# A new order for the first tiles and block one of a chunk-attention and elu-FFN kernel, and three single steps moved later

## The chip, the cores and the metric

The kernel runs on one core of one Trainium2 chip. The metric is the device time of one launch in microseconds (us). Each kernel is run several times; the median of the runs stands for it. One further execution is recorded by the hardware profiler, and all rows quoted below come from it.

## What is computed

Two stages, both in float32. First attention inside chunks of 64 tokens (batch 8, 8 heads, 576 tokens, head size 64), then a feed-forward layer with an elu between two products:

```
scores = scale * q_c @ k_c^T            # per chunk of 64 tokens
attn   = softmax(scores)                # exp(scores - max) / (sum + 1e-9)
x      = (attn @ v_c) as [4608, 512]    # tokens by (head, dim)
h      = x @ w_in                       # w_in  [512, 2048]
g      = where(h > 0, h, exp(min(h, 0)) - 1)
out    = g @ w_out                      # w_out [2048, 512]
```

q, k and v are float32. The two weights reach the kernel as 64-bit floats, seen as pairs of 32-bit words.

## The kernel before

**Blocks and tiles.** The 4608 tokens are nine blocks of 512 (TB); a block is four tiles of 128 (P). Blocks 0 to 2 are done plainly; blocks 3 to 8 are done in three pairs with a seven-product scheme. The change is in block 0 ("block one" in the words of the change), in what comes ahead of it, and at three places behind it.

**Products.** TensorE multiplies in a fast float32 form that keeps fewer bits, so each operand is split into a high part and the rest, and each product is three matmuls (`three`, L419: high by high, high by low, low by high). `hidden(f)` (L428) makes one 128x512 tile of h from four slices of the contraction: 12 matmuls. One hidden slice f of 16 then goes through `elu` (L436), a generator with four steps, each an "e" in the order strings: ScalarE takes relu and exp (L439, L440); VectorE joins them with a maximum (L442); ScalarE casts the high part ghi (L447); VectorE subtracts to get glo (L450). Then four groups of three matmuls add the slice to the four output tiles (`second_products`, "P", 12 matmuls). So one f is "H", four "e" and one "P".

**Weights.** In blocks 0 and 1 the split weights are used from SBUF, and block 0 must make them. A unit u (`load_unit`, L109) is slice u of w_in and slice u-1 of w_out, 512 KB each, loaded into one of three `st` buffers (the first unit has w_in alone, the last w_out alone). Per unit ScalarE runs two steps ("r", `prepare_units`, L135 and L140), VectorE runs a clamp (L164) and two bit operations (L171, L177), with two casts on ScalarE behind the last (L184) ("d", `split_units`), and VectorE subtracts for each part (L155). H of slice f needs unit f; P of slice f needs unit f+1. A buffer is free for unit u+3 when unit u has passed L177.

**Attention of the first eight tiles.** `early_attention` (L265) is a generator with ten steps: transposes of q and k on TensorE (L271), two copies on ScalarE (L278), scores on TensorE (L249), maximum on VectorE, exp on ScalarE, sum and division on VectorE (L306 to L309), turning on TensorE (L316), a copy (L323), the product with v on TensorE (L257), and putting x away. "By head" the exp is eight small instructions that also return sums (L294); else VectorE subtracts the maximum (L300), one exp follows (L304), and VectorE sums (L306). In the first block's tiles x is put away by a cast to xhi and a subtraction to xlo (L413, L414), both read by every H.

**What sets the order.** TensorE, ScalarE, VectorE and the SyncE queue run in the order in which the program issues instructions: the schedule is manual. Strings of one-letter items write that order out. `LOADS` gives the order of the first loads, all issued ahead of `START`; `START` interleaves tiles 0 to 3 with the first weight steps ("w13" and "w10" are matmuls of the identity, digits are a tile's next step); `FIRST_BLOCK` has one line for each of four f's in turn, "a" being the next step of the running tile (tiles 4 to 7, all by head). SyncE issues every load and store, so a load that waits for its buffer holds the loads behind it. `split_upto(f)` forces the weight steps that H needs. At the end of block 0, "X" splits the next block's x into xhi and xlo (L849, L850), and GpSimd begins sums for the later blocks (`combine`, L480).

The three later places are in `THIRD_BLOCK` (block 2; "q" and "k" are VectorE's transpositions of the next tile's q and k, L348; "xT2b" prepares an operand named T2), and in `KEPT` (the second block of each pair; "m" is attention's maximum, "4" is a step of an elu, L587 then L590; "G" splits a slice of g that was kept, L595 and L597).

Of the kernel before, what the change touches and what calls it, by code (L numbers as in the profile page):

```python
# [20 lines left out]
def kernel(  # L21
# [124 lines left out]
    def split_units():  # L146
# [6 lines left out]
        def subtract(u: int):  # L153
            for (hi, lo), w in before:
                nc.vector.tensor_tensor(out=lo, in0=w, in1=hi.bitcast(F32), op=ALU.subtract)  # L155
                yield
            split.append(u)

        before = []
        for u in range(NU):  # L160
            low, high, parts = units[u]
            highf = high.bitcast(F32)
            need(u, "high")
            nc.vector.tensor_scalar(  # L164
                out=highf, in0=highf, scalar1=LARGEST, scalar2=-LARGEST, op0=ALU.min, op1=ALU.max
            )
            yield
            need(u, "low")
            y = ybuf[u % 2].bitcast(U32).rearrange(
                "p (i a t) -> p i a t", i=2, a=4)[:, :len(parts)]  # L170
            nc.vector.scalar_tensor_tensor(  # L171
                out=y, in0=high, scalar=3, in1=low, op0=ALU.logical_shift_left, op1=ALU.bitwise_or
            )
# [8 lines left out]
            before = [(part, y[:, i].bitcast(F32)) for i, part in enumerate(parts)]  # L182
            for (hi, _), w in before:
                nc.scalar.copy(out=hi, in_=w)  # L184
            yield
            if u <= 1:
                yield from subtract(u)
        yield from subtract(NU - 1)

    preparation = prepare_units()  # L190
    split = []
    splitting = split_units()

    def split_upto(u: int):
        while u not in split:
            next(splitting)
# [68 lines left out]
    def early_attention(tt: int, q_sb, k_sb, v_sb, kT, at, a_pool, pool, put, by_head: bool):  # L265


        both = pool.tile([P, 2, DM], F32, name="ps_a")
# [57 lines left out]
        multiply_v(x_ps, v_sb, aT.rearrange("p h (u t) -> p u h t", u=2))  # L326
# [101 lines left out]
    def hidden(f: int):  # L428
        hi, lo = w_in_slices(f)
        h = ps_h.tile([P, TB], F32, name="h")  # L430
        for kt in range(NK):
            three(h, hi[:, kt, :], lo[:, kt, :], xhi[:, kt, :], xlo[:, kt, :],
                  kt == 0, kt == NK - 1)
# [285 lines left out]
    def warm(n: int):  # L719

        warm_ps = ps_start.tile([P, 2, DM], F32, name="ps_a")[:, 0, :].rearrange(
            "p (i t) -> p i t", i=4)
# [11 lines left out]
    FIRST_BLOCK = (  # L734
# [63 lines left out]
    )  # L798
    PRELOADED = sum(item[0] == "u" for item in LOADS.split())

# [9 lines left out]
    with (  # L810
# [4 lines left out]
        loaded = {}  # L815
        for item in LOADS.split():
            kind, n = item[0], int(item[1:])
            if kind == "u":
                load_unit(n)
            else:  # L820
                loaded[item] = load_heads(
                    {"q": q, "k": k, "v": v}[kind], f"{kind}_sb", n * P, start)
        tiles = [early_attention(
            tt, *[loaded[f"{kind}{tt}"] for kind in "qkv"],
            start.tile([P, NK, P], F32, name="kT"), start, start, ps_start, split_first_x,
            tt in BY_HEAD,
        ) for tt in range(NTT)]
        for item in START.split():
            if item[0] == "w":
                warm(int(item[1:]))  # L830
            else:
                next({"d": splitting, "r": preparation}.get(item) or tiles[int(item)])

    wo1 = ctx.enter_context(tc.tile_pool(name="wo1", bufs=1))
    later_w_out = w_out_tiles(wo1)
    gp = ctx.enter_context(tc.tile_pool(name="gp", bufs=2))
    plain = ctx.enter_context(ExitStack())
    wi1 = plain.enter_context(tc.tile_pool(name="wi1", bufs=1))
    weights.append((*w_in_tiles(wi1), *later_w_out))
    io = plain.enter_context(tc.tile_pool(name="io", bufs=2))  # L840
    ps_h = ctx.enter_context(tc.tile_pool(name="ps_h", bufs=2, space=bass.MemoryType.PSUM))
    ps_o = ctx.enter_context(tc.tile_pool(name="ps_o", bufs=1, space=bass.MemoryType.PSUM))
    early = ctx.enter_context(ExitStack())
    ps_early = early.enter_context(
        tc.tile_pool(name="ps_early", bufs=1, space=bass.MemoryType.PSUM))
# [7 lines left out]
    def early_tile(n: int):  # L853
# [3 lines left out]
                  for src, name, pool in ((q, "q_sb", io), (k, "k_sb", io), (v, "v_sb", vio))]  # L857
        return early_attention(
            n % NTT, *loaded, k_turned, at, wi1, ps_early, lambda tt, src: keep_x(tt, src), True)
# [14 lines left out]
    following = early_tile(NTT)  # L874
    for blk in range(PLAIN - 1):
        if blk == 1:
            early.close()
            ps_a = ctx.enter_context(
                tc.tile_pool(name="ps_a", bufs=1, space=bass.MemoryType.PSUM))
        run = blk * TB, o_tiles(), None  # L880
        for f in range(NF):
            tt, st = divmod(f, 4)
            n = (blk + 1) * NTT + tt + 1
            if st == 0:
                if (blk, tt) == (1, 0):
                    following = later[2 * NTT].steps()
                tile_now, following, begun = following, iter(()), 0
                if blk:
                    next(tile_now, None)
                    next(tile_now, None)  # L890
                    if tt == 0:
                        later[n] = Later(n)
                        later[n].load_qk()
                    later[n].load_v()
                    following = later[n].steps()
            lines = FIRST_BLOCK if blk == 0 else SECOND_BLOCK if (blk, tt) == (1, 0) else LATER
            for item in (LAST if blk and f == NF - 1 else lines[st]).split():
                if item == "H":
                    if blk == 0:
                        split_upto(f)  # L900
                        if f == NF - 1:
                            kept_st += [stp.tile([P, STAGE], F32, name="kept", tag="st")
                                        for _ in range(3)][::-1]
                            later[2 * NTT] = Later(2 * NTT)
                            later[2 * NTT].load_qk()
                            later[2 * NTT].load_v()
                    act, acted = elu(hidden(f)), 0
                elif item == "e":
                    g, acted = next(act), acted + 1
                    if acted == 4:  # L910
                        second(f, *g)
                elif item == "a":
                    next(tile_now, None)
                    begun += 1
                    if begun == 2 and n < 2 * NTT:
                        following = early_tile(n)
                elif item == "n":
                    next(following, None)
                elif item == "d":
                    next(splitting, None)  # L920
                elif item == "r":
                    next(preparation, None)
                elif item[0] == "X":
                    if f == NF - 1:
                        split_next(*[int(kt) for kt in item[1:]])
                elif item == "P":
                    if blk or f:
                        second_products()
                elif item == "S":
                    store(*unstored.pop())  # L930
            if (blk or f > 1) and (not blk or f < 2):
                write_lo((f - 2) % NF)
            if blk:
                next(combining, None)
                if st == 2:
                    later[n + 1] = Later(n + 1)
                    later[n + 1].load_qk()
# [107 lines left out]
```

## Time and profile before

| | us |
|---|---|
| median of 3 runs | 846.59 (845.35 to 848.22) |
| profiled execution, own time | 848.72 |
| its span, first to last instruction | 846.7 |
| TensorE busy (matmul records) | 829.1 (98%) |
| VectorE / ScalarE / GpSimd busy | 501.2 / 483.7 / 176.5 |
| moved by DMA | 164.10 MB, 194 GB/s on the mean |

The span is what the rows cover; the execution's own time has 2.0 us more around it, and that execution stands 2.1 us above the median. Matmul records overlap, since a matmul's record is longer than the distance to the next start, so busy time does not show what TensorE could save; distances between starts do. In rows of the timeline the first number is the start in us, the second the duration; a bracket gives idle time of that engine ahead of the row and what released it. PE is TensorE, DVE VectorE, ACT ScalarE, POOL GpSimd, SPq the SyncE queue.

### The profile page before, as it was taken

Reading aid. Unit: us, or ns where it says so; the run is one execution under the profiler, and the core shown is the slowest. Engines: PE = TensorE matmul, PEld = TensorE weight load, DVE = VectorE, ACT = ScalarE, POOL = GpSimd, SP = SyncE. Lnnn points to the kernel's source line nnn. Section 1 sums busy time; section 2 is a strip of 40 time slices with the busy share of each in tenths; the row PEclk is TensorE's granted clock in tenths of the full one; section 3 lists DMA queues with packets and bytes.
Section 4 is the critical chain, followed back from the end, with each engine's and each line's share of the span. In section 5 each row is a group of like instructions: output and inputs, shape, how many; then the busy total and the mean of one; then the engine's idle time right before and its main releaser. Section 6 shows DMA issues by size and latency. Waiting matters only on the chain.

```text
span 846.7 us, 15737 instructions
## 1 busy us (share of the span) xinstructions
PE 829.1 (98%) x5959; PEld 678.1 (80%) x5959; DVE 501.2 (59%) x717; ACT 483.7 (57%) x855; POOL 176.5 (21%) x148
## 2 busy tenths in 40 slices
PE   6899999999999999999999999999999999999998
PEld 5687887888878887888888888788888888888786
DVE  5888996666775769666666745666555333233411
ACT  6799985544564547656656436556664355555521
POOL 0000005355302120211113531111126211111120
PEclk9799999999999999999999999999999999999999
DMA  9877672767768786698887656798854365545231
GB/s 240 259 214 228 220 223 75 223 201 240 240 191 229 207 220 183 185 252 247 236 257 243 183 151 208 197 257 242 225 159 137 109 195 162 164 142 161 92 108 50
DMA packets 178795, 164.10 MB, mean 194 GB/s; under 512 B 65568, under 2 KB 161312, under 8 KB 178720
## 3 DMA queue, kind: packets, MB, share of 16 engines
q1 hardware_dynamic: 178720, 163.10, 66.0%
q8 instruction: 47, 0.77, 0.4%
q14 instruction: 28, 0.23, 0.1%
HBM read 131.07 MB, written 28.31 MB: 188 GB/s over the span
## 4 chain that ended last, share of the span: by engine, by line
PE 90%; ACT 3%; DMA 2%; DVE 2%; SPq 1%; issue 1%; DVEq 0%; ACTq 0%
PE o L422 44%; PE h L422 41%; PE ps_a L249 2%; PE ps_a L257 2%; SPq L213 1%; DMA k_sb<-in_k_dram 1%; PE ps_a L316 1%; DMA v_sb<-in_v_dram 1%; DMA wi_hi<-a_dram 1%; DMA turned<-unturned 0%; DVE g_kept L590 0%; PE ps_a L271 0%; ACT e L440 0%; ACT e L587 0%; DVE xlo L850 0%
## 5 line engine op out<-in xcount | busy, mean ns | idle before, releaser
L422 PE MATMUL o<-wo_hi,ghi 128*128 128x512 f32 x416 | 165.4, 398 | 0.0
L422 PE MATMUL o<-wo_hi,glo 128*128 128x512 f32 x416 | 163.1, 392 | 0.2 <-DMA wi_hi<-a_dram 0.2
L422 PE MATMUL o<-wo_lo,ghi 128*128 128x512 f32 x416 | 162.8, 391 | 0.0
L597 POOL TENSOR_TENSOR glo<-e,ghi 128x512 fp32r<-128x512 f32 x46 | 59.6, 1296 | 317.3 <-ACT ghi L595 311.8
L422 PE MATMUL h<-xhi,wi_hi 128*128 128x512 f32 x336 | 112.1, 392 | 0.1
L422 PE MATMUL h<-xlo,wi_hi 128*128 128x512 f32 x336 | 111.4, 390 | 0.7 <-DVE xlo L850 0.7
L422 PE MATMUL o<-wo_hi,wo_lo 128*128 128x512 f32 x320 | 99.8, 390 | 1.0 <-DVE kept L455 1.0
L422 PEld LDWEIGHTS o<-wo_hi,ghi 128*128 128x128 f32 x416 | 78.6, 189 | 17.4 <-ACT ghi L447 0.2
L422 PEld LDWEIGHTS o<-wo_hi,glo 128*128 128x128 f32 x416 | 78.5, 189 | 17.5 <-DVE glo L450 1.0
L422 PEld LDWEIGHTS o<-wo_lo,ghi 128*128 128x128 f32 x416 | 78.6, 189 | 15.8
L636 ACT COPY kept<-h 128x512 f32<-128x512 f32 x72 | 42.3, 588 | 61.6 <-PE h L422 61.6
L422 PE MATMUL h<-wi_lo,wi_hi 128*128 128x512 f32 x288 | 75.0, 396 | 0.0
L422 PE MATMUL h<-xhi,wi_lo 128*128 128x512 f32 x192 | 74.9, 390 | 0.0
L422 PEld LDWEIGHTS h<-xlo,wi_hi 128*128 128x128 f32 x336 | 63.1, 188 | 14.0 <-DVE xlo L850 1.1
L422 PEld LDWEIGHTS h<-xhi,wi_hi 128*128 128x128 f32 x336 | 63.1, 188 | 13.6 <-PE ps_a L724 0.3
L422 PE MATMUL h<-wo_lo,wi_hi 128*128 128x512 f32 x288 | 73.0, 389 | 0.0
L422 PEld LDWEIGHTS o<-wo_hi,wo_lo 128*128 128x128 f32 x320 | 60.1, 188 | 14.4 <-DVE kept L455 1.9
L590 DVE SCALAR_TENSOR_TENSOR g_kept<-e,g_kept 128x512 f32<-128x512 f32 x48 | 35.5, 739 | 57.7 <-ACT e L587 57.7
L640 DVE TENSOR_TENSOR g_kept<-h,kept 128x512 f32<-128x512 f32 x48 | 33.1, 689 | 51.7 <-ACT kept L636 27.2
L422 PEld LDWEIGHTS h<-wo_lo,wi_hi 128*128 128x128 f32 x288 | 54.1, 188 | 11.2
L587 ACT ACTIVATE e<-e 128x512 f32<-128x512 f32 x96 | 60.7, 633 | 3.1
L422 PE MATMUL o<-wo_lo 128*128 128x512 f32 x160 | 62.3, 389 | 0.0
(107 smaller groups left out, 1318.0 us busy)
## 6 DMA issues: line engine op xcount, KB each, us to landing
wi_hi<-a_dram SPq DMA_DIRECT2D x168, 256.0 KB, 3.9
wo_lo<-lo_dram SPq DMA_DIRECT2D x52, 512.0 KB, 4.7
kept<-in_q_dram SPq DMA_DIRECT2D x100, 128.0 KB, 3.4
kept<-in_k_dram SPq DMA_DIRECT2D x100, 128.0 KB, 3.8
st<-in_moe_w_in_dram SPq DMA_DIRECT2D x16, 512.0 KB, 4.9
v_sb<-in_v_dram SPq DMA_DIRECT2D x32, 256.0 KB, 5.8
st<-in_moe_w_out_dram SPq DMA_DIRECT2D x16, 512.0 KB, 5.3
a_dram<-kept SPq DMA_DIRECT2D x16, 512.0 KB, 4.0
```

Source lines behind the costliest of these rows:

```text
L213: nc.sync.dma_start(out=dst[p0:p0 + n], in_=src[b, :, s0:s0 + n, :].rearrange("h s d -> s h d"))
L249: nc.tensor.matmul(scores[halves[c], j, hp, :], lhsT=qT[halves[j], hp, halves[c]], rhs=kT[halves[j], hp, halves[c]], start=True, stop=True,)
L257: nc.tensor.matmul(x_ps[halves[j], c, hp, :], lhsT=v_sb[halves[c], 2 * hp + j, :], rhs=aT[halves[c], :, j * NK + hp], start=True, stop=True,)
L316: nc.tensor.matmul(turned_ps[half, h, :], lhsT=a[half, h, :], rhs=ident[half, half], start=True, stop=True,)
L422: nc.tensor.matmul(ps, lhsT=a, rhs=b, start=start, stop=stop, skip_group_check=onto)
L587: nc.scalar.activation(out=e, in_=e, func=AF.Exp, scale=-1.0)
L590: nc.vector.scalar_tensor_tensor(out=to, in0=e, scalar=-1.0, in1=c, op0=ALU.add, op1=ALU.max)
L597: engine.tensor_tensor(out=lo, in0=e, in1=hi.bitcast(F32), op=ALU.subtract)
L636: nc.scalar.copy(out=c21 if i == 4 else self.kept[i - 1], in_=x_ps)
L640: nc.vector.tensor_tensor(out=to, in0=y_ps, in1=self.kept[kept], op=ALU.add)
```

## The change

Tile and weight steps are no longer tied to f. One string gives the order of block 0 item by item, loads and subtractions included ("u3" loads a unit, "L4" a tile's q, k, v, "s" is one subtraction of L155, "l0" writes a low part out, "K" loads for the next block).

- `START` holds the loads too, in another order: v0 ahead of q2, all v ahead of u0. The ten identity matmuls "w10" ahead of the first H are gone. By head are tiles 2, 4 and 5 (before: 3 to 7).
- The first H runs its 12 matmuls in the order high by high, low weights by xhi, high weights by xlo.
- Before the end of block 0, P of slice 13 and P of slice 14 both follow the last H; X follows, and a one-column GpSimd copy of xlo holds GpSimd's sums until xlo is done.
- Some tile pools get `reuse_waits="tile"`.
- `THIRD_BLOCK` line 0: "q" moves ahead of the second "e"; line 15: the last "e" (glo) ahead of "xT2b". `KEPT` line 0: the second "4" moves ahead of G and E.

```
-            if u > 2:
-                yield from subtract(u - 1)
...
-            if PRELOADED <= u + 2 < NU:
-                load_unit(u + 2)
...
+            for i, (hi, _) in enumerate(parts):
+                nc.scalar.copy(out=hi, in_=y[:, i].bitcast(F32))
+                merged.append((parts[i], y[:, i].bitcast(F32)))
+    def subtract_next():
+        (hi, lo), w = merged.pop(0)
+        nc.vector.tensor_tensor(out=lo, in0=w, in1=hi.bitcast(F32), op=ALU.subtract)

     def hidden(f: int):
...
+        if f:
...
+        else:
+            terms = [(w, xhi, kt) for w in (hi, lo) for kt in range(NK)]
+            terms += [(hi, xlo, kt) for kt in range(NK)]

-    LOADS = "q0 k0 q1 k1 q2 k2 u0 q3 k3 v0 v1 u1 v2 v3"
-    BY_HEAD = (3,)
+    BY_HEAD = (2, 4, 5)
     START = (
-        "w13 0 1 0 1 0 0 1 0 2 2 2 1 3 0 r 0 1 1 3 3 1 r 0 0 2 3 2 d 1 3 d d 2 r 3 1 2 d 3 d 2 0 "
-        "3 2 1 2 3 w10 3 r d d d d r r d"
+        "q0 k0 q1 k1 w13 v0 0 1 0 q2 0 k2 q3 0 k3 1 1 v1 0 2 v2 1 3 0 2 2 v3 1 2 3 u0 3 1 2 u1 0 "
+        "r r 1 3 1 0 3 2 2 d u2 d 1 0 r d 3 3 2 s 2 0 r d 1 d 3 r 2 3 3"
     )
     FIRST_BLOCK = (
-        "r H e d e a r e a d d e P",
-        "d H a e d a a e e d r r d a e P d",
-        "d H d e r e a e d a r d e P d",
-        "r H d a e d d e r a e d d e d X P d",
+        "H r u3 r d L4 d e s 4 d 4 e e s r d e u4 H d s 4 e s r P e 4 d e e H 4 e d 4 L5 e s u5 d "
+        "P e e u6 r r 4 d 4 s H r e 4 d 4 d r l0 e e s r d u7 d s e d P u8 5 s d H P e r 5 L6 e e "
...
+        "e P s e e H d e e s e e d l11 H P e e d K l12 P s X e l13 e"
     )

     THIRD_BLOCK = {
-        0: "h H e e P l V e S q k e",
+        0: "h H e q e P l V e k S e",
-        15: "H s v e x V e xt1b xt3b xT1b e xt2b xT2b e xt4b",
+        15: "H s v e x V e xt1b xt3b xT1b e xt2b e xT2b xt4b",
     KEPT = (
-        "4 m G E 4 Q Q Q Q G",
+        "4 m 4 G E Q Q Q Q G",

+        elif item == "X":
+            split_next()
+            nc.gpsimd.tensor_copy(out=kept_st[1][:, :1], in_=xlo[:, NK - 1, :1].bitcast(F32))
```

More of the change, by code (lines that the diff above doesn't have):

```diff
@@ L828, with start_banks, start_step @@
[L828 to L834, printed above, removed]
+        loaded, tiles, warmed = {}, {}, []
+        def start_banks():
+            return ps_start.tile([P, 2, DM], F32, name="ps_a")
+        def start_step(item: str):
+            tt = int(item)
+            if tt not in tiles:
+                tiles[tt] = early_attention(
+                    tt, *[loaded[kind, tt] for kind in "qk"], lambda: loaded["v", tt],
+                    start.tile([P, NK, P], F32, name="kT"), start, start,
+                    lambda: start_banks() if tt else warmed[0],
+                    split_first_x, tt in BY_HEAD)
+            next(tiles[tt])
@@ L872 @@
     kept_st, unstored, banks, later, t3_place = [], [], [], {}, []
[L874 to L937, printed above, removed]
@@ new lines @@
+    run, f, early_tiles = (0, o_tiles(), None), -1, {}
+    for item in FIRST_BLOCK.split():
+        if item == "H":
+            f += 1
+            act, acted = elu(hidden(f)), 0
+        elif item == "e":
+            g, acted = next(act), acted + 1
+            if acted == 4:
+                second(f, *g)
+        elif item == "P":
+            second_products()
+        elif item[0] == "L":
+            early_tiles[item[1]] = early_tile(int(item[1]))
+        elif item in early_tiles:
+            next(early_tiles[item])
+        elif item == "d":
+            next(merging)
+        elif item == "s":
+            subtract_next()
+        elif item == "r":
+            next(preparation)
+        elif item[0] == "u":
+            load_unit(int(item[1:]))
+        elif item[0] == "l":
+            write_lo(int(item[1:]))
+        elif item == "K":
+            kept_st += [stp.tile([P, STAGE], F32, name="kept", tag="st") for _ in range(3)][::-1]
+            later[2 * NTT] = Later(2 * NTT)
+            later[2 * NTT].load_qk()
+            later[2 * NTT].load_v()
+        elif item == "X":
+            split_next()
+            nc.gpsimd.tensor_copy(out=kept_st[1][:, :1], in_=xlo[:, NK - 1, :1].bitcast(F32))
```

125 lines of the change are left out of this document (79 added, 46 removed), and 4 rows, old and new, of the table FIRST_BLOCK.

## The prediction

> **What bounds the kernel now.** I read the page first, then the timeline of TensorE (PE) for the distances between starts, then what ScalarE (ACT) did while PE stood.
>
> ```profile
> PEclk9799999999999999999999999999999999999999
> PE 90%; ACT 3%; DMA 2%; DVE 2%; SPq 1%; issue 1%; DVEq 0%; ACTq 0%
> ```
>
> PE is on 90% of the chain that ended last, so the order of the other engines is worth only what PE loses by it: time before its first H, stretches without a start, and the second slice's clock, where a 7 stands among nines. The PE timeline shows all three in the first 43 us.
>
> ```profile
> 17.54 0.69 PE L257 MATMUL ps_a<-qT,v_sb 64*64 64x64 f32 x32 [0.27 <-ACT qT L323]
> 20.59 2.67 PE L316 MATMUL ps_a<-ident,a 64*64 64x64 f32 x62 [2.35 <-DVE a L309]
> 26.74 0.47 PE L422 MATMUL h<-xhi,wi_hi 128*128 128x512 f32 x1
> 33.05 0.39 PE L422 MATMUL h<-xhi,wi_lo 128*128 128x512 f32 x1
> 37.40 1.14 PE L249 MATMUL ps_a<-k_turned,qT 64*64 64x64 f32 x32 [3.97 <-ACT k_turned L278]
> 39.48 0.63 PE L422 MATMUL o<-wo_hi,glo 128*128 128x512 f32 x1
> 39.91 0.63 PE L422 MATMUL o<-wo_hi,ghi 128*128 128x512 f32 x1
> 52.29 0.39 PE L422 MATMUL h<-xlo,wi_hi 128*128 128x512 f32 x1
> 52.51 0.39 PE L422 MATMUL h<-xhi,wi_lo 128*128 128x512 f32 x1
> 65.46 0.69 PE L249 MATMUL ps_a<-k_turned,qT 64*64 64x64 f32 x32
> 133.32 0.40 PE L422 MATMUL h<-xhi,wi_hi 128*128 128x512 f32 x1
> 134.45 0.50 PE L422 MATMUL h<-xlo,wi_hi 128*128 128x512 f32 x1 [0.73 <-DVE xlo L850]
> ```
>
> A big matmul starts every 0.23 us at full clock (52.29 to 52.51) and every 0.43 us in the slow stretch (39.48 to 39.91). H of slice 0 starts at 26.74. After H of slice 1 PE stands from 33.28 to 37.40, 4.12 us, for the copies of tile 4's transposed q and k. At the end of block 0 it stands 0.90 us for xlo (133.32 to 134.45, less 0.23). Between 43 and 133 us I found no distance between starts beyond those of the attention steps: there the block is bound by PE.
>
> The clock, by windows (after the span of a window: its length, busy time and count of each engine, then the granted clock):
>
> ```profile
> 22.00:24.00 2.00, 2.00 (x62) 2.00 (x57) 1.48 (x3) 1.46 (x4) 0.00 (x0) 0.54 1.01 379
> 24.00:26.00 2.00, 2.00 (x44) 1.82 (x40) 1.39 (x3) 1.73 (x5) 0.00 (x0) 0.61 1.09 376
> 34.00:36.00 2.00, 0.00 (x0) 0.00 (x0) 1.10 (x2) 1.97 (x4) 0.00 (x0) 0.95 0.99 306
> 36.00:38.00 2.00, 0.60 (x23) 0.60 (x25) 2.00 (x4) 2.00 (x5) 0.00 (x0) 0.50 0.55 207
> 40.00:42.00 2.00, 2.00 (x6) 1.56 (x5) 1.97 (x5) 1.43 (x10) 0.00 (x0) 0.50 0.53 207
> 42.00:46.00 4.00, 4.00 (x17) 3.04 (x15) 3.40 (x7) 4.00 (x13) 0.00 (x0) 0.92 0.41 122
> ```
>
> If the clock is either whole or half, 0.54 and 0.61 make 2 x (0.92 + 0.78) = 3.4 us at half clock, behind an idle time of 2.36 us (17.54 + 0.69 to 20.59). The second stretch is 0.2 + 3 x 2 + 0.64 = 6.8 us (38 to 40 also shows 0.50), behind the stall of 4.12 us. So PE pays twice for that stall: ten matmuls at 0.20 us too much, 2.0 us, and the scores at 37.40 take 1.14 in place of 0.69 (65.46), 0.45 us.
>
> **The start, until H of slice 0.** What ACT runs here:
>
> ```profile
> 13.36 0.66 PE L271 MATMUL ps_a<-ident,k_sb 128*128 128x128 f32 x4 [0.44 <-DMA k_sb<-in_k_dram]
> 15.01 0.69 ACT L140 ACTIVATE st<-st 128x512 uint32<-128x512 uint16 x1
> 17.38 0.32 ACT L294 ACTIVATE a<-ps_a,mx 128x64 f32<-128x64 f32 x1
> 19.71 0.66 ACT L184 CAST wi_hi<-xf 128x512 fp32r<-128x512 f32 x1
> 30.00 0.61 ACT L184 CAST wo_hi<-xf 128x512 fp32r<-128x512 f32 x1
> 30.52 1.14 ACT L135 ACTIVATE st<-st 128x1024 f32<-128x1024 f32 x1
> 31.56 1.13 ACT L140 ACTIVATE st<-st 128x1024 uint32<-128x1024 uint16 x1
> 34.24 0.63 ACT L440 ACTIVATE e<-e 128x512 f32<-128x512 f32 x1
> 34.77 1.11 ACT L140 ACTIVATE st<-st 128x1024 uint32<-128x1024 uint16 x1
> 36.29 0.57 ACT L278 COPY qT<-ps_a 128x512 f32<-128x512 f32 x1
> 36.77 0.58 ACT L278 COPY k_turned<-ps_a 128x512 f32<-128x512 f32 x1
> ```
>
> From start to start: a cast 0.52, a whole weight step 1.04, an exp 0.53, a copy 0.48, the eight exps by head 2.33 (17.38 to 19.71). Tile 3's k is the ninth load in either order, so its transposes stay near 13.4, its copies end near 15.1, and the eight exps (tile 2's now) near 17.5. Next in ACT's queue stands unit 0, whose load has moved from seventh to thirteenth place, behind all of v: 3.5 MB in all. Before, 3.5 MB were reached with the first half of unit 1:
>
> ```profile
> L114 SPq DMA_DIRECT2D st<-in_moe_w_in_dram x1: 582/582/582, 12.7 to 12.7; - x1
> DMA to landing us min/median/max: 5.1/5.1/5.1
> ```
>
> That is 17.8. ACT, in order, then runs two half-size steps (0.6 each), an exp (0.53), three whole weight steps (3.1), one cast (0.52), four copies (1.9) and the four casts to xhi (like the copies, 1.9): 9.2 us, which ends at 27.0. Units 1 and 2 are later in the queue too, and I allow 0.7 us for waits on them and for the last cast to finish: H at 27.7, 1.0 us later than 26.74. Bounds: 26.7 (ACT finds its data each time) and 28.7. The three whole steps are no loss in themselves: before, only the first of them was done when H started, and 2.1 us of ACT's work come out of what follows. The new order of terms hides xlo: the last subtraction (0.6 behind the last cast) has eight matmuls, 1.8 us, to finish.
>
> The ten identity matmuls that filled PE up to H are gone, and by this chain PE has only tile 3's product with v (0.69) between some 24.2, when tile 2's product ends behind its copy, and 27.7. Idle time of 2.36 us was enough for 3.4 us of half clock, so I expect about one such stretch inside H: 3.4 us carry half the work, a loss of 1.7. Bounds: 0, and 3.4 for a stretch like the second one.
>
> [...]
>
> **The first slices of block 0.** ACT is what made PE wait: from 30.52 to 36.29 whole weight steps of units 2 and 3 stood ahead of elu 0, ghi and tile 4's copies. In the new order unit 1 and half of unit 2 are through, the copies stand directly behind elu 0's exp, and only two whole steps (unit 2 low, unit 3 high) and two casts lie between the last xhi and relu. Worked forward from H at 27.7 with the steps above: H0 ends 32.2, tile 4's transposes 33.1, its copies 34.4, H1 35.9; the scores follow at once; glo 0 is ready at 36.4 and P0 starts at 36.6; wi_lo 2 is ready at 37.6 and H2 starts at 39.3. No stall stays, the tightest place being P0 with 0.2 us. What hides tile 4's copies is H1 (2.7 us). Gone are 4.12, 2.0 and 0.45: 6.6 us.
>
> **The rest of block 0.** The work per slice is the same, except that tiles 6 and 7 lose 1.8 us each on ACT (2.33 for 0.53) and gain 1.2 on DVE (two passes of 0.6). The cover:
>
> ```profile
> 78.50:104.17 25.67, 25.67 (x202) 20.74 (x201) 23.51 (x34) 23.64 (x50) 0.00 (x0) 1.00 0.77 237
> ```
>
> In four slices DVE (23.51) and ACT (23.64) leave 2.0 us of 25.67, 0.5 per slice. The distances between an H and the subtraction that it needs are about one slice in the new order, so I put this part at nothing. At the end, P13 and P14 (2.7 each) follow the last H and cover relu and exp (0.6 each), four casts to xhi (1.9) and the first subtraction (0.6), some 4 us: the stall of 0.90 goes. Next would be glo 15, with a further 2.7 us of H ahead of its P.
>
> **The three later places.** The stalls there, and DVE at the last:
>
> ```profile
> 236.87 0.69 PE L249 MATMUL ps_a<-k_turned,qT 64*64 64x64 f32 x32 [0.54 <-DVE k_turned L348]
> 330.13 0.50 PE L422 MATMUL o<-wo_hi,glo 128*128 128x512 f32 x1 [0.18 <-DMA wi_hi<-a_dram]
> 635.59 0.50 PE L422 MATMUL o<-wo_hi,wo_lo 128*128 128x512 f32 x1 [0.35 <-DVE kept L455]
> 799.81 0.50 PE L422 MATMUL o<-wo_hi,wo_lo 128*128 128x512 f32 x1 [0.67 <-DVE kept L455]
> 796.74 0.69 DVE L597 TENSOR_TENSOR wo_lo<-g_kept,wo_lo 128x512 fp32r<-128x512 f32 x1 [1.01 <-ACT wo_lo L595]
> 797.35 1.80 DVE L590 SCALAR_TENSOR_TENSOR g_kept<-e,g_kept 128x512 f32<-128x512 f32 x1
> ```
>
> With the usual distance taken off they are 0.70, 0.33, 0.51 and 0.83 us. q goes into DVE's wait for elu 0's exp, and k is then ready before the scores; glo moves ahead of a subtraction that no matmul needs for 3 us (the DMA named at 330.13 only lands near). In KEPT the maximum goes into DVE's idle 1.01 us, where it takes 0.69 in place of 1.80, and the copies that PE waits for come earlier. I count all four: 2.4 us; bounds 0 and 2.4.
>
> **Sum.** +1.0 +1.7 -6.6 -0.9 -2.4 = -7.2 us. The profiled execution would go from 848.7 to 841.5; it stands 2.1 above the median, so from 846.6 I come to 839.4.
>
> **Rivals.**
> The clock stays whole at the first H: gaps under 2 us each do not halve it. Against it stands the half clock behind 2.36 us; for it, that each gap here is shorter. 837.7. [...]
> The stall only moves: tile 4's loads stand behind unit 3, whose buffer waits for unit 0's L177, near 20.5 by the chain above; if q and k land 2 to 3 us after H0, PE stands in front of H1 and gets a second stretch at half clock. That gives back 2.5 + 1.7 to 3.4, and the time is 843.6 to 845.3. For it: unit 1's load took 5.1 us to land, so little is spare. Against it: up to k of tile 4 the queue holds 3.5 MB behind unit 0, which at some 300 GB/s (306 to 379 in the windows above) are 12 us, so they land near 30, ahead of H0's end at 32.2.
> The later places give nothing, because the next wait there ends as late: 841.8.
> Slower: weight loads bind block 0. A unit's load needs the buffer that L177 frees three units earlier, and "r" waits for it in ACT's queue with relu behind it. If each of 12 slices overran the 0.5 us of slack by 0.9, that is 10.8, and the time is 850.2; it decides from 0.6 us per slice (7.2). against it: a load landed in 5.1 us when the queue was full, three slices last 19 (25.67 x 3/4), and PE did not stand after 43 us.
> That the change does not do what it says would mean reordered strings that leave PE's waits: only the second rival has a place for that.
>
> **How the numbers follow.** The forecast has 0.52, the whole clock 0.22, nothing at the later places 0.10, the moved stall 0.11, the slower case 0.05. Low end: whole clock, H at 26.7 and a little more, 836.5. High end: H at 28.7, the longer half clock (+1.0, +1.7) and part of the later places missing, 843.5. A measurement of this kernel can tell about 0.3% from no change, 2.5 us: faster means below 844.1. The forecast, the whole clock, the later places, and a third of the moved stall lie there: 0.87; the rest of the moved stall and some of the slower case make 0.09; slower 0.04.
>
> **What would show it.** Right: first H near 27.7 with a clock of about 0.5 in some 3.4 us from there, no distance over 1 us between starts from 33 to 43, the first H of block 1 near 129 without a bracket for xlo, and the four later brackets gone. Wrong: a bracket for a DMA or for wi_lo ahead of H1 or P0, a second stretch at half clock, or ACT waiting for weight loads in the middle of block 0.

## The result, and the profile after

| | before | after |
|---|---|---|
| median, us | 848.39 (845.35 to 849.93, 6 runs) | 840.68 (838.51 to 841.98, 6 runs) |
| profiled execution, own time | 848.72 | 841.98 |
| its span | 846.7 | 840.2 |
| first H of block 0 starts | 26.74 | 28.88 |
| H of slice 2 starts | 43.25 | 38.92 |
| first H of block 1 starts | 133.32, then stands 0.90 for xlo | 128.96 |

The ratio is 0.9908 [0.9887, 0.993], so the change takes 7.7 us off (5.9 to 9.6): faster, as forecast (7.2). In rows of after the lines of the code are others: L408 is the matmul of `three`, L425 that of the first H with its own order of terms, L235 the scores, L243 the product with v, L257 the transposes, L302 the turning, L264 and L309 copies, L399 and L857 casts to xhi, L400 the subtraction to xlo, L270 and L276 the maximum, L280 the exps by head, L295 the division, L172 the casts of the weights, L443 glo, L717 the matmuls of the identity.

The page of after, the granted clock in 40 slices and the shares of the chain that ended last:

```profile
PEclk8999999999999999999999999999999999999999
PE 92%; ACT 2%; DVE 2%; DMA 2%; SPq 1%; issue 1%; DVEq 0%; ACTq 0%
```

The 7 in the second slice is gone; an 8 stands in the first. PE has 92% of the chain for 90%. The timeline of PE in after, from the last product of tile 3 on:

```profile
26.86 0.69 PE L243 MATMUL ps_a<-qT,v_sb 64*64 64x64 f32 x32 [0.26 <-ACT qT L309]
28.88 1.19 PE L425 MATMUL h<-xhi,wi_hi 128*128 128x512 f32 x4 [1.32 <-ACT xhi L399]
32.18 0.60 PE L257 MATMUL ps_a<-ident,k_sb 128*128 128x128 f32 x4
32.53 0.48 PE L408 MATMUL h<-xhi,wi_hi 128*128 128x512 f32 x1
35.44 0.69 PE L235 MATMUL ps_a<-k_turned,qT 64*64 64x64 f32 x32
36.07 0.50 PE L408 MATMUL o<-wo_hi,ghi 128*128 128x512 f32 x1
38.92 0.39 PE L408 MATMUL h<-xhi,wi_hi 128*128 128x512 f32 x1
128.96 1.07 PE L425 MATMUL h<-xhi,wi_hi 128*128 128x512 f32 x4
130.78 1.07 PE L425 MATMUL h<-xlo,wi_hi 128*128 128x512 f32 x4
135.12 0.50 PE L408 MATMUL h<-xhi,wi_hi 128*128 128x512 f32 x1
```

Behind 28.88 no row has a bracket up to the start of block 1. The scores of tile 4 follow H1 directly, where PE had stood 4.12 us; P0 follows the scores, and H of slice 2 comes 10.0 us after the first H, where it took 16.5 before. At 130.78 the part with xlo starts without a wait. What stayed is one idle time ahead of the first H, which now begins 2.14 us later than before.

### The profile page after: what moved, and what is told of

Same layout as the page of the kernel before. It is cut to its first block, busy times and chain, and to the rows that moved or that the text cites. A ratio compares the mean times of both kernels' runs of the same rounds, so it can differ in the third digit from the quotient of the medians.

```text
span 840.2 us, 15685 instructions
## 1 busy us (share of the span) xinstructions
PE 826.3 (98%) x5949; PEld 677.0 (81%) x5949; DVE 501.6 (60%) x719; ACT 480.4 (57%) x825; POOL 179.0 (21%) x149
## 4 chain that ended last, share of the span: by engine, by line
PE 92%; ACT 2%; DVE 2%; DMA 2%; SPq 1%; issue 1%; DVEq 0%; ACTq 0%
PE o L408 45%; PE h L408 40%; PE ps_a L235 2%; PE ps_a L243 2%; PE h L425 1%; DMA turned<-unturned 1%; SPq L199 1%; DMA k_sb<-in_k_dram 1%; PE ps_a L257 1%; PE ps_a L302 1%; SPq L373 0%; ACT st L135 0%; ACT a L280 0%; DVE e L435 0%; ACT e L433 0%
## 5 line engine op out<-in xcount | busy, mean ns | idle before, releaser
L408 PE MATMUL o<-wo_hi,ghi 128*128 128x512 f32 x416 | 163.8, 394 | 0.1
L408 PE MATMUL o<-wo_hi,glo 128*128 128x512 f32 x416 | 162.2, 390 | 0.0
L408 PE MATMUL o<-wo_lo,ghi 128*128 128x512 f32 x416 | 162.0, 390 | 0.0
L408 PE MATMUL h<-xhi,wi_hi 128*128 128x512 f32 x324 | 108.1, 394 | 0.0
L408 PE MATMUL h<-xlo,wi_hi 128*128 128x512 f32 x324 | 106.7, 389 | 0.0
L408 PE MATMUL o<-wo_hi,wo_lo 128*128 128x512 f32 x320 | 99.2, 389 | 0.0
L408 PEld LDWEIGHTS o<-wo_hi,ghi 128*128 128x128 f32 x416 | 78.1, 188 | 17.4 <-ACT ghi L440 0.5
L408 PEld LDWEIGHTS o<-wo_hi,glo 128*128 128x128 f32 x416 | 78.1, 188 | 16.7 <-DVE glo L443 0.4
L408 PEld LDWEIGHTS o<-wo_lo,ghi 128*128 128x128 f32 x416 | 78.1, 188 | 15.8
L408 PE MATMUL h<-wi_lo,wi_hi 128*128 128x512 f32 x288 | 75.0, 396 | 0.0
L408 PE MATMUL h<-wo_lo,wi_hi 128*128 128x512 f32 x288 | 72.9, 389 | 0.0
L408 PEld LDWEIGHTS h<-xhi,wi_hi 128*128 128x128 f32 x324 | 60.8, 188 | 12.9
L408 PEld LDWEIGHTS h<-xlo,wi_hi 128*128 128x128 f32 x324 | 60.8, 188 | 12.2
L408 PEld LDWEIGHTS o<-wo_hi,wo_lo 128*128 128x128 f32 x320 | 60.1, 188 | 12.5
L408 PE MATMUL h<-xhi,wi_lo 128*128 128x512 f32 x180 | 70.2, 390 | 0.0
L583 DVE SCALAR_TENSOR_TENSOR g_kept<-e,g_kept 128x512 f32<-128x512 f32 x48 | 33.2, 692 | 61.4 <-ACT e L580 61.4
L408 PEld LDWEIGHTS h<-wo_lo,wi_hi 128*128 128x128 f32 x288 | 54.1, 188 | 11.2
L408 PE MATMUL o<-wo_lo 128*128 128x512 f32 x160 | 62.2, 389 | 0.0
```

The costliest lines, as they stand in the source:

```text
L408: nc.tensor.matmul(ps, lhsT=a, rhs=b, start=start, stop=stop, skip_group_check=onto)
L583: nc.vector.scalar_tensor_tensor(out=to, in0=e, scalar=-1.0, in1=c, op0=ALU.add, op1=ALU.max)
```

## Experiments

Two theories were to be told apart. The first is the forecast's: ScalarE's queue (ACT) makes PE wait in the opening, the order of block 0 removes that, and the other places add their own small gains. The second: what counts is how early the first H starts and whether the clock is whole there, so that the remaining 2.1 us and more are still to be had by a better start. Medians of one group are compared with the kernel before as it ran beside them: 848.46 for e0 to e3, 847.61 for e4, e5, e6 and e8, 847.40 for e7, e9, e10 and e11. The changed kernel itself ran only beside the first of these groups (e0), so the later ones are set against it by their ratios too.

**e0: the changed kernel again**, for the spread between executions.

> The changed kernel once more, on the chip of the next three, so that they are compared with it there. Both theories expect what was measured: a ratio of 0.991 to the kernel before (about -7.7 us). Its profile also tells whether the half clock inside the start falls at the same place again (14 to 20 us) or somewhere else.

840.36 us (838.8 to 841.82), 0.9905 [0.9886, 0.9924]; first H at 28.77, H of slice 2 at 38.85, block 1 at 128.9. Against after the opening repeats to 0.1 us. Its six runs go from 838.8, with a mean granted clock of 1.000 on record, to 841.82 with 0.994. The span of its profile is 837.9, 2.3 less than that of after; the difference lies behind block 0 and is taken up with the ledger below.

**e1: the three later places alone**, in the kernel before.

```
-        0: "h H e e P l V e S q k e",
+        0: "h H e q e P l V e k S e",
-        15: "... e xt2b xT2b e xt4b",
+        15: "... e xt2b e xT2b xt4b",
-        "4 m G E 4 Q Q Q Q G",
+        "4 m 4 G E Q Q Q Q G",
```

> The kernel before with the three later places alone (q ahead of the maximum in block 2, glo ahead of T2's low part, the maximum ahead of the casts in KEPT). Theory: the four stalls of 0.70, 0.33, 0.51 and 0.83 us are each a loss of their own at the end of the kernel, so this is 2.4 us faster than before. Rival: what follows waits as late by another way and the opening of block 0 carries the whole gain: 0 to -0.5 us.

846.0 us, 0.9969 [0.9957, 0.9982]: 2.46 us less (1.5 to 3.6). All four stalls are gone from its trace. Two of them in rows, the scores behind the moved q and VectorE's (DVE's) maximum ahead of the casts:

```profile
235.96 0.69 PE L249 MATMUL ps_a<-k_turned,qT 64*64 64x64 f32 x32
793.33 0.69 DVE L590 SCALAR_TENSOR_TENSOR g_kept<-e,g_kept 128x512 f32<-128x512 f32 x1 [0.50 <-ACT e L587]
```

Neither place has a next wait that ends as late: the scores have no bracket, and the maximum takes 0.69 where it had taken 1.80. The 2.4 of the forecast is shown, within that interval; by subtraction the rest, about 5 us, comes from the start and block 0.

**e2: P of slice 13 back ahead of the last H**, so that one P covers the split of the next x.

```
-... e e d l11 H P e e d K l12 P s X e l13 e"
+... e e d l11 P H e e d K l12 P s X e l13 e"
```

> The changed kernel with P of slice 13 moved back ahead of the last H, so that one P and not two covers relu, exp, the casts to xhi and the subtractions to xlo. Theory (cover): in the changed kernel the first cast to xhi starts 3.4 us after the last H ends, and one P is 2.7 us, so the first H of block 1 waits; with casts every 0.52 us against matmuls every 0.23 us that is 1.5 to 2.2 us slower than the changed kernel. Rival (GpSimd): the old stall came from GpSimd's sums that slowed VectorE, and they are held by the one-column copy here, so it is at most 0.3 us slower.

843.03 us, 0.9937 [0.9916, 0.9958]: 2.67 above e0. Its timeline and its clock by windows (after the window: its length, the busy times of PE, weight loads, DVE, ACT and GpSimd, then the granted clock):

```profile
28.87 1.27 PE L425 MATMUL h<-xhi,wi_hi 128*128 128x512 f32 x4 [1.33 <-ACT xhi L399]
29.93 1.91 PE L425 MATMUL h<-xhi,wi_lo 128*128 128x512 f32 x4
34.12 0.47 PE L408 MATMUL h<-xhi,wi_hi 128*128 128x512 f32 x1
40.53 0.39 PE L408 MATMUL h<-xhi,wi_hi 128*128 128x512 f32 x1
132.29 2.06 PE L425 MATMUL h<-xhi,wi_hi 128*128 128x512 f32 x4 [1.13 <-ACT xhi L857]
139.49 0.50 PE L408 MATMUL h<-xhi,wi_hi 128*128 128x512 f32 x1
```

```profile
28.00:30.00 2.00, 1.13 (x5) 0.93 (x6) 1.64 (x3) 2.00 (x4) 0.00 (x0) 0.97 0.32 66
30.00:32.00 2.00, 2.00 (x6) 1.60 (x5) 1.92 (x3) 1.96 (x3) 0.00 (x0) 0.50 0.66 145
32.00:34.00 2.00, 2.00 (x11) 1.57 (x10) 1.30 (x2) 0.41 (x1) 0.00 (x0) 0.68 0.93 282
```

At the end of the block PE now waits 1.13 us for the casts to xhi, and the four matmuls behind it take 2.06 where they took 1.07 in after. Waiting for each cast would give that (an estimate: four casts take 2.18 us from 126.87 on in after, three steps of some 0.52 and a matmul of 0.50 make 2.06); the clock there is not shown. From H of slice 2 to the second H of block 1 it takes 98.96 us (40.53 to 139.49), in after 96.20 (38.92 to 135.12), so the second P is worth 2.8 us in this trace. The one-column GpSimd copy stayed, so what it adds is not shown. The first rows show something else, and by chance, since the program up to there is that of after: here the clock is half for 0.12 + 2 + 1.28 = 3.4 us at the first H, and H1 starts at 34.12, 1.6 us later than in after. That is the term the forecast put at 1.7, in an execution where it fell. So the median's 2.67 could hold a share of the clock as well. The record of the single runs speaks for a small one: at a mean granted clock of 1.000 e2 took 841.29 and e0 838.8, again 2.5 us apart.

**e3: tile 2's scores, maximum and exps ahead of tile 3's transposes**, against the wait for tile 3's k, which landed at 13.86 in after.

```
-... 1 v1 0 2 v2 1 3 0 2 2 v3 1 2 3 u0 3 1 2 u1 0 r r 1 3 1 0 3 2 2 d u2 ..."
+... 1 v1 0 2 v2 1 0 2 2 v3 1 2 0 3 1 2 u0 3 3 1 u1 2 1 0 3 2 2 3 r r d u2 ..."
```

> The changed kernel with another START: tile 2's scores, maximum and exps ahead of tile 3's transposes, which wait for the ninth load, and the attention copies of tiles 0 to 2 ahead of unit 0's steps on ScalarE. Theory: between 12 and 17 us ScalarE and VectorE stand behind PE's wait for that load (3.8 and 3.2 us idle), and from 20 to 46 us both are full, so what is idle there is lost at the end; the first H comes at 25 to 26 in place of 28.9, but units 1 and 2 land no earlier (21.6 and 24.2 us), so 0.5 to 2.5 us faster than the changed kernel. Rival 1: the start of the first H sets the end, so 3 to 4 us faster. Rival 2: loads alone set the opening, so no difference.

842.02 us, 0.9925 [0.9908, 0.9943], 1.7 above e0 where 0.5 to 2.5 less was expected. Tile 3 became late instead: PE waits 4.73 us for its probabilities (25.70, below), the first H starts at 30.43.

```profile
25.70 1.85 PE L302 MATMUL ps_a<-ident,a 64*64 64x64 f32 x30 [4.73 <-DVE a L295]
30.43 1.21 PE L425 MATMUL h<-xhi,wi_hi 128*128 128x512 f32 x4 [1.02 <-ACT xhi L399]
```

**e4, e5, e6: an earlier first H.** e4 moves one weight step of ACT behind the last tile's copies. e5 gives the whole start another order (tile 2 ahead of tile 3, weight steps later). e6 adds to e5 that H1 comes before tile 4's transposes.

```
e4:
-... r d 1 d 3 r 2 3 3"
+... r d 1 d 3 2 3 3 r"
e5, from v2 on:
+"... v2 1 0 2 2 v3 1 2 0 3 1 1 2 u0 3 3 u1 2 2 1 0 r r 3 3 2 d u2 d 1 0 3 3 0 1 r 3 d s d 2 2 3 3 r d r"
e6, also:
-"H r u3 r d L4 d e s 4 d 4 e e s r d e u4 H d s 4 e s r P e 4 d e e H ..."
+"H r u3 d L4 d e s r d e e s e H 4 4 r P d u4 4 d s e s r e 4 d e e H ..."
```

> The changed kernel with unit 2's first weight step behind the last cast to xhi on ScalarE, so that the first H starts 1.04 us earlier (27.8 in place of 28.8). Theory: the opening is bound by the sum of ScalarE's and VectorE's work, not by the first H; the step comes back ahead of unit 1's casts, and H of slice 1 waits for its low part, which is ready only 0.35 us ahead of it now, so 0 to 0.4 us faster than the changed kernel. Rival: what starts earlier ends earlier, 1.0 us faster.

> The start of e3 mended: tile 3's division ahead of unit 0's bit operations on VectorE, tile 1's turning ahead of tile 3's scores on TensorE, and tile 3's copy ahead of unit 0's cast. First H near 25.7 in place of 28.8. Theory (work of ScalarE and VectorE): H of slice 1 is then held by unit 1's low part (about 30.1) and by tile 4's transposes ahead of it, whose k lands near 31, so it starts at 31 to 32 in place of 32.5: 0.5 to 1.5 us faster than the changed kernel. Rival 1: 3 us faster, with the first H. Rival 2: no difference, since e3 gained nothing.

> e5 with tile 4's transposes moved behind H of slice 1 and its scores behind P of slice 0, and unit 3's first step behind unit 1's casts. H of slice 1 then waits for no load, only for unit 1's low part near 30.1. Theory: 1.5 to 2.5 us faster than the changed kernel, 1 us faster than e5. Rival: unit 3 and tile 4 are late further on by the same time, so no faster than e5.

Measured: e4 840.13 us, 0.9918 [0.9905, 0.9931]; e5 842.58, 0.9943 [0.9927, 0.9959]; e6 841.98, 0.9938 [0.9923, 0.9952]. Each started the first H earlier, by 0.6, 1.8 and 1.0 us, and none is faster than the changed kernel; e5 and e6 look slower, by 1.3 to 2.2 us in medians and some 3 us in ratios. Each trace has another place where the lead went. In e4:

```profile
28.28 1.20 PE L425 MATMUL h<-xhi,wi_hi 128*128 128x512 f32 x4 [0.70 <-ACT xhi L399]
32.76 0.63 PE L257 MATMUL ps_a<-ident,k_sb 128*128 128x128 f32 x4 [0.85 <-DMA k_sb<-in_k_dram]
```

In e5:

```profile
22.51 0.68 PE L302 MATMUL ps_a<-ident,a 64*64 64x64 f32 x16 [2.75 <-DVE a L295]
27.10 2.07 PE L425 MATMUL h<-xhi,wi_hi 128*128 128x512 f32 x4 [0.70 <-ACT xhi L399]
32.03 0.60 PE L257 MATMUL ps_a<-ident,q_sb 128*128 128x128 f32 x4
31.18 1.14 ACT L135 ACTIVATE st<-st 128x1024 f32<-128x1024 f32 x1 [0.97 <-DMA st<-in_moe_w_out_dram]
```

In e6:

```profile
32.12 0.50 PE L408 MATMUL h<-xhi,wi_hi 128*128 128x512 f32 x1 [1.23 <-ACT wi_hi L172]
43.93 0.50 PE L408 MATMUL o<-wo_hi,glo 128*128 128x512 f32 x1 [0.88 <-DVE glo L443]
```

e4 meets tile 4's k, which lands just then. e5 ran its first H at half clock (0.50 between 26 and 30; 2.07 for four matmuls, 1.19 in after), so that the transposes behind it began at 32.03, in after at 31.74. In both ACT itself stands for a weight load behind the first H, 0.42 us at 30.73 in e4 and 0.97 us at 31.18 in e5, which after's ACT does not. e6, at a whole clock (1.20 for the four matmuls at 27.87), found neither the cast of wi_hi nor, later, glo. An early first H alone is thus not what the end of block 0 hangs on.

**e8: tile 4's copies behind two more weight steps**, one part of the change undone inside block 0.

```
-"H r u3 r d L4 d e s 4 d 4 e e s r d e u4 H ..."
+"H r u3 r d L4 d e s 4 d e e s r d 4 e u4 H ..."
```

> The changed kernel with the suspected cost put back: tile 4's two copies behind one whole weight step and two casts on ScalarE (u3's second step, unit 2's casts). Theory: PE stands 2.0 us between H of slice 1 and tile 4's scores (the copies end at 37.5 in place of 34.2, H of slice 1 ends at 35.4), and perhaps runs at half clock behind it, so 2.0 to 3.7 us slower than the changed kernel. Rival: the opening is bound by the sum of ScalarE's work and the order of one copy does not matter: 0 to 0.5 us slower.

844.99 us (842.01 to 846.01, 10 runs), 0.9968 [0.9956, 0.998]: 4 to 5 us above the changed kernel in the other groups, above what was expected. The stall is back:

```profile
31.44 0.60 PE L257 MATMUL ps_a<-ident,k_sb 128*128 128x128 f32 x4
37.18 0.69 PE L235 MATMUL ps_a<-k_turned,qT 64*64 64x64 f32 x32 [2.40 <-ACT k_turned L264]
```

```profile
36.00:38.00 2.00, 0.82 (x33) 0.75 (x34) 1.39 (x3) 1.97 (x5) 0.00 (x0) 1.00 1.07 251
38.00:40.00 2.00, 2.00 (x10) 1.60 (x9) 1.64 (x4) 1.92 (x4) 0.00 (x0) 1.00 1.01 373
```

This execution was the fastest of its ten, and in it the clock stays whole behind 2.40 us of idle time; H of slice 2 starts at 40.7, 1.8 us later than in after, behind a first H that came 0.7 us sooner. The other nine runs are 2 to 4 us slower. Their mean granted clock on record is 0.994 to 0.996, against 1.000 in this one, so they did run at a lower clock. No profile shows where in the run, so that it lay behind the stall is argued and not shown. At 1.000 the changed kernel took 838.8 (a run of e0), 3.2 us less than this one. Shown is that the position of the copies in ACT's order makes this stall.

**e7, e9, e10: identity matmuls in the gaps ahead of the first H**, meant to keep the clock whole, in the changed kernel (e7), in e5 (e9) and in e6 (e10).

```
e7:
-... r d 1 d 3 r 2 3 3"
+... r d 1 w8 d 3 r 2 3 w10 3"
e9 and e10, in the start of e5:
-... 3 3 0 1 r 3 d s d 2 2 3 3 r d r"
+... 3 3 0 1 w8 r 3 d s d 2 2 3 w8 3 r d r"
```

> The changed kernel with identity matmuls in two of TensorE's waits ahead of the first H (8 ahead of tile 3's product with v, 10 ahead of H); no other work moves. In one of three profiles of kernels with this start (e2) the first H ran at half clock, in two it did not. Theory (clock): a busy TensorE ahead of H leaves the clock whole at H in each execution, which takes the slow executions away: 0.3 to 1 us faster on the median and a narrower spread than 838.5 to 842. Rival: the half clock in the start costs nothing, since ScalarE and VectorE set the pace there: no difference, within 0.3 us.

> e5 (842.58 us, first H at 27.1 but at half clock from 24.6 to 31.2) with identity matmuls ahead of tile 2's product with v and ahead of the first H. Theory (clock): e5's earlier H was eaten by the half clock, which its longer idle stretch of 2.75 us brought about; with TensorE busy from 23 to 27 the clock is whole again by the first H or soon behind it, so 1.5 to 3 us faster than e5. Rival: e5 is slow for another reason (glo of slice 0, VectorE's work), so within 0.5 us of e5.

> e6 (841.98 us) with the same identity matmuls. e6's profile had a whole clock at H, a wait of 1.2 us for unit 1's cast and one of 1.0 us for glo of slice 1. Theory (clock): what the median has above the profiled execution is half clock, so 0.5 to 1.5 us faster than e6; its two waits stay. Rival: no difference to e6.

e7: 839.63 us (838.74 to 840.54), 0.9911 [0.9896, 0.9926]. Its clock is whole from 18 us on (1.00 in each window to 46), the first H at 29.0, slice 2 at 39.04: not to be told from the changed kernel. Its five runs lie closer (1.8 us against 3.5), but the gain of 0.3 to 1 us that was expected is less than these runs can tell, so this question stays open. e9: 842.1, 0.9937 [0.9922, 0.9953]; e10: 842.64, 0.9948 [0.9932, 0.9964]: a miss for both, since e9 stands 0.5 below e5 and e10 0.7 above e6. In e9 the clock was half before the added matmuls came (0.52 between 22 and 24, 0.50 to 28), and the first eight took 1.97 us, in PE's order ahead of the product with v; in e10 it was 0.56 and 0.59 between 24 and 28. In e9:

```profile
24.70 1.97 PE L717 MATMUL ps_a<-ident 128*128 128x128 f32 x8
28.51 1.27 PE L717 MATMUL ps_a<-ident 128*128 128x128 f32 x8
29.93 1.16 PE L425 MATMUL h<-xhi,wi_hi 128*128 128x512 f32 x4
```

The first H came at 29.93 in place of e5's 27.10.

**e11: the first H in the old order of terms**, three by three, so that its second matmul needs xlo.

```
-        if f:
-            ...
-        else:
-            terms = ...
+        for kt in range(NK):
+            three(h, hi[:, kt, :], lo[:, kt, :], xhi[:, kt, :], xlo[:, kt, :], kt == 0, kt == NK - 1)
```

> The changed kernel with the old order of the 12 terms in the first H of a block (high by high, high by low, low by high for each slice). The last cast to xhi ends at 28.8 and the last subtraction to xlo at 29.7, so the second matmul waits 0.6 to 0.8 us in block 0, and H ends about as much later. Theory (ScalarE and VectorE set the opening): 0.2 to 0.5 us of it is taken up by the wait for unit 1's low part that follows, so 0.2 to 0.6 us slower in block 0; block 1 has xlo in time: nothing. Rival: the whole 0.8 us, and more in block 1.

840.94 us, 0.9927 [0.9909, 0.9944], not to be told from the changed kernel. The wait is there:

```profile
28.20 0.50 PE L408 MATMUL h<-xhi,wi_hi 128*128 128x512 f32 x1 [1.31 <-ACT xhi L399]
29.04 0.50 PE L408 MATMUL h<-xlo,wi_hi 128*128 128x512 f32 x1 [0.34 <-DVE xlo L400]
32.50 0.48 PE L408 MATMUL h<-xhi,wi_hi 128*128 128x512 f32 x1
```

In this execution the first H came 0.7 us sooner than in after, and H1 at 32.50 against 32.53, so between the two H it took 4.3 us for 3.65. The old order cost 0.65 us here, and the earlier start hid it. At the end of the block it lost nothing either (128.9): there xlo had the time of two P.

**All starts together.** Times in us; ACT's idle time is 26 less its busy time in the window from 12 to 38.

| kernel | first H | H of slice 2 | first H of block 1 | ACT idle, 12 to 38 | ratio |
|---|---|---|---|---|---|
| e0 | 28.8 | 38.9 | 128.9 | 3.20 | 0.9905 |
| e11 | 28.2 | 38.9 | 128.9 | 3.41 | 0.9927 |
| after | 28.9 | 38.9 | 129.0 | 3.86 | 0.9908 |
| e7 | 29.0 | 39.0 | 129.1 | 4.04 | 0.9911 |
| e4 | 28.3 | 39.6 | 129.7 | 4.25 | 0.9918 |
| e5 | 27.1 | 40.1 | 130.1 | 4.94 | 0.9943 |
| e3 | 30.4 | 40.5 | 130.6 | 4.95 | 0.9925 |
| e8 | 28.1 | 40.7 | 130.7 | 3.68 | 0.9968 |
| e6 | 27.9 | 39.6 | 130.9 | 5.64 | 0.9938 |
| e9 | 29.9 | 41.5 | 131.6 | 6.11 | 0.9937 |
| e10 | 29.9 | 41.1 | 132.5 | 7.01 | 0.9948 |

Two rows of that window, after and then e10:

```profile
12.00:38.00 26.00, 20.11 (x396) 17.30 (x397) 22.14 (x38) 22.14 (x49) 0.00 (x0) 0.87 0.92 267
```

```profile
12.00:38.00 26.00, 21.13 (x378) 17.80 (x379) 20.54 (x37) 18.99 (x43) 0.00 (x0) 0.87 0.82 250
```

PE is busier in e10 (21.13 against 20.11) and the kernel is slower; ACT has 3.2 us less done by 38, and block 1 starts 3.5 us later. Down the table block 1 comes 90.04 us behind H of slice 2, 91.37 in e6 and e10 alone, whose order of block 0 differs: what is lost by slice 2 is not made good. Block 1 also goes with ACT's idle time, about 1 us for 1 us, and not with the first H: 27.1 gives 130.1, and 28.9 gives 129.0. e8 falls out of this second rule: its ACT was busy, but with other work than the copies that PE waited for. What the second theory expected did not come in these starts: e4, e6 and e11 began the first H 0.6 to 1.0 us sooner, at a whole clock (1.00 from 20 to 38 in e4 and from 18 to 46 in e11; four matmuls in 1.20 us in e6), and H of slice 2 came 0.7 later, 0.7 later and at the same time.

That ACT's lost time is the cause of the column is a correlation. A half clock also goes with more idle time of ACT: e2, the program of after up to there, had a half clock at the first H (0.50 between 30 and 32), and its ACT stood 4.95 us, 1.59 of them between 32 and 34, and its H of slice 2 came at 40.5; ACT stood 3.20 in e0 and 3.86 in after. ACT's waits for weight loads in e4 and e5 make the loads a candidate too. No run held the clock and the loads and changed ACT's work alone. Nor does any run undo `reuse_waits`, the choice of tiles by head or the GpSimd copy.

## Why the prediction was right, step by step

The forecast of 839.4 stands against 840.68, and -7.2 against -7.7 (5.9 to 9.6). The difference is the fairer comparison, since 839.4 was counted from a median of 3 runs, 846.59, which is 848.39 over 6. The mechanism was right; two terms at the first H were off in opposite directions, 1.1 us too little and 1.7 too much, so that the sum came as close as it did is in part luck.

**First H, +1.0: mis-sized, +2.14**, 0.2 past the upper bound of 28.7. The step that failed is the start of ACT's chain, "That is 17.8". The timeline of after:

```profile
13.86 1.12 PE L257 MATMUL ps_a<-ident,k_sb 128*128 128x128 f32 x4 [1.91 <-DMA k_sb<-in_k_dram]
14.91 2.37 PE L235 MATMUL ps_a<-kT,qT 64*64 64x64 f32 x64
16.18 0.69 DVE L270 TENSOR_REDUCE mx<-ps_a 128x8 f32<-128x512 f32 x1 [3.22 <-ACT kT L264]
17.18 0.31 ACT L280 ACTIVATE a<-ps_a,mx 128x64 f32<-128x64 f32 x1 [1.09 <-DVE mx L276]
19.50 0.70 ACT L135 ACTIVATE st<-st 128x512 f32<-128x512 f32 x1
```

In PE's order tile 2's scores stand behind tile 3's transposes of k, and those waited for their load until 13.86. Then came scores at half clock, a maximum, and only at 17.18 the exps, which the forecast had finished by 17.5; unit 0's step ran at 19.50. I had let the exps follow ACT's copies, without what they need from PE and DVE. But that is not the only limit. In e2, whose program is the same up to there, k landed 0.9 us sooner (12.97) and the exps began at 15.39, and then ACT waited for the load itself, and again later for tile 3:

```profile
18.84 0.67 ACT L135 ACTIVATE st<-st 128x512 f32<-128x512 f32 x1 [0.97 <-DMA st<-in_moe_w_in_dram]
26.20 0.59 ACT L309 COPY qT<-ps_a 128x512 f32<-128x512 f32 x1 [0.51 <-PE ps_a L302]
```

So unit 0 was to be had at 18.8 and not at 17.8, and the first H still came at 28.87. The 9.2 us of ACT's work were right (19.50 + 9.2 = 28.7 against 28.88 in after, where ACT never stands behind 19.5), and so was the 0.7 allowed for waits (18.84 + 9.2 + 0.7 = 28.7 against 28.87 in e2). e3 shows that the order of tiles 2 and 3 cannot simply be turned.

**Half clock at the first H, +1.7: in some executions.** It was nothing in after, e0, e4, e7, e8 and e11, whose first H runs at a whole clock in the profiles (four matmuls in some 1.2 us; 1.00 from 18 to 46 in e11), and 1.6 in e2 with the same program up to there. The windows of after show where it went:

```profile
12.00:14.00 2.00, 0.14 (x1) 0.14 (x2) 0.90 (x2) 0.33 (x1) 0.00 (x0) 0.81 0.84 186
14.00:16.00 2.00, 2.00 (x36) 1.52 (x36) 0.00 (x0) 0.98 (x2) 0.00 (x0) 0.50 0.89 192
18.00:20.00 2.00, 2.00 (x40) 1.89 (x38) 1.93 (x4) 2.00 (x13) 0.00 (x0) 0.50 1.06 390
20.00:24.00 4.00, 2.64 (x114) 2.39 (x110) 3.72 (x10) 4.00 (x8) 0.00 (x0) 0.99 0.75 286
28.00:32.00 4.00, 3.12 (x15) 2.57 (x16) 3.91 (x6) 3.98 (x6) 0.00 (x0) 1.00 0.71 156
```

It begins within the wait for k that ends at 13.86 (0.81 between 12 and 14), and by 20 it is over. So the case "the clock stays whole" is what these profiles show at the first H, but not for its reason, the gaps under 2 us: that wait is 1.91 us, and e2's half clock at H follows a gap of 1.33 us, and from 20 to 26 PE's idle time there is 1.56 us in all. Its -8.9 was missed by 1.2 us, what the first H came later than the 27.7 of its sum.

**The opening of block 0, -6.6: right.** From first H to H of slice 2 the forecast had 27.7 to 39.3, 11.6 us, of which 1.7 were half clock; without it 9.9. Measured 10.0. e8 shows that the position of tile 4's copies makes or removes the stall. "The stall only moves" was near: in e4, where the first H ended half a microsecond sooner, PE waited 0.85 us for tile 4's k, which the forecast had landing near 30 and which PE got at 32.7 there.

**The rest of block 0 at nothing: right.** Block 1 starts 90.04 us behind H of slice 2, before 90.07 (43.25 to 133.32). From slice 2 to block 1 neither PE nor ACT waits for a load in after, so the slower rival's mechanism did not appear.

**The end of block 0, -0.9: right.** No wait at 130.78 in after; with one P less, a wait of 1.13 us and 2.06 us for four matmuls in place of 1.07 (e2). First H of block 1 "near 129": 128.96.

**The three later places, -2.4: right by themselves** (-2.46 in e1), but the profile of after alone does not show it. Its span is 6.5 us shorter, and 5.26 of that are there by block 1 (133.32 and the 0.90, less 128.96). The four brackets are gone, worth 2.4; against that PE waits longer for one DMA of attention, here in after:

```profile
540.94 1.03 PE L243 MATMUL ps_a<-turned,v_sb 64*64 64x64 f32 x32 [0.79 <-DMA turned<-unturned]
558.67 0.69 PE L243 MATMUL ps_a<-turned,v_sb 64*64 64x64 f32 x30 [0.34 <-DMA turned<-unturned]
```

With 0.26 at 558.04 these brackets are 1.39 us, and they cost more: from the scores of one tile to those of the next it takes 16.28 us without such a wait (506.89 to 523.17), here 17.63 and 17.39, 2.46 us in all. The kernel before had one such wait, 0.44 at 546.89, which cost 1.03; e0, the same program as after, had no bracket and 0.14. Against before that is 1.43 lost, and -5.26 - 2.4 + 1.43 makes -6.2 of the 6.5. So the waits come and go between executions, and they are the whole 2.3 us between the spans of after and e0. The profiled execution was also the slowest of the six; the median is the fairer figure, and it agrees with the sum.

## What to carry over

Where an engine with an order of its own feeds the bound engine through an opening, look at how long that feeder stands idle and at what it does first, and not only at how early the first large piece of work starts: here a first H up to 1.8 us earlier gained nothing, and two copies put behind other work (e8) made the bound engine stand 2.40 us. When you work a chain forward, give every step the inputs that it needs from the loads and the other engines' queues too, above all where two tiles stand one behind the other in one of them. And a gain of a few microseconds is judged by medians: the same program differed by 2.3 us between two profiled spans.

## What was not expected of the hardware

In these profiles the stretches at half clock worked out here last 3.4 us or twice that, estimated from the granted clock of the windows as either whole or half: 3.4 in e0 (0.56 and 0.59 between 14 and 18 make 2 x (0.88 + 0.82)) and in e2's second one (0.97, 0.50 and 0.68 above: 0.12 + 2 + 1.28), 6.8 in after (0.76 + 6 + 0.08) and in e5 (0.69, 0.50, 0.50 and 0.60 between 24 and 32: 1.24 + 4 + 1.6). Where one falls differs between executions of programs that are the same up to there: after has it from about 13 to 20 us, e0 from 14 to 18, e2 from 20 to 23 and again from 30 to 33. In e5 it stands behind an idle time of 2.75 us; behind the 2.40 of e8 it stayed away. Ahead of the first H, 1.33 us of idle time in e2 were followed by a half clock, and 1.33 us in e0 were not.
